# Softmax division of three batches moved to ScalarE and GpSimd with one folded factor, and an earlier start of some weight sums, in a fused attention and feed-forward kernel

## The chip, the cores and the metric

The kernel runs on one core of a Trainium2 chip. A core has a matrix engine (TensorE, PE in the profile, whose weight loads are listed as PEld), a vector engine (VectorE, DVE), a scalar engine (ScalarE, ACT), GpSimd (POOL) and SyncE (SP), which here issues the DMA transfers. The metric is device time in microseconds, as the median of several executions. One further execution is taken with the hardware profiler, and all rows below come from it.

## What is computed

Four batches of eight heads of causal attention with a memory term are computed, and the result goes, as 2304 tokens of 512 features, through two gated feed-forward blocks. All data are fp32. Cut to what matters:

```python
# attention, per batch and head: S = 576, D = 64
scores = where(causal, -1e9, q @ k.T / sqrt(D))
a = exp(scores - scores.max(-1));  a /= a.sum(-1) + 1e-9
local = a @ v
q_p = phi(q)                                  # elu(q) + 1
mem_out = (q_p @ M_prev) / (q_p @ z_prev + 1e-6)
g = 1 / (1 + exp(-beta))                      # one number per head
x = g * mem_out + (1 - g) * local             # 2304 x 512
# block 1: w1, w2 512x1024, w3 1024x1024, w_out 1024x512
x = ((x @ w1) * (x @ w2)) @ w3 @ w_out
# block 2: w_gate, w_val 512x1536, w_out 1536x512
out = (sigmoid(x @ w_gate) * (x @ w_val)) @ w_out
```

## The kernel before

**Batches and overlap.** The work goes batch by batch. `attention(b)` is a generator over 4 pairs of heads `p` and 5 row tiles `i` of 116 rows; row tile `i` sees 116(i+1) columns because of the causal mask, so its probabilities are 116x116 up to 116x580. `ffn(b)` is a generator over the feed-forward blocks of batch b. `drive` alternates the steps of `ffn(b)` with those of `attention(b+1)`, so the attention of batches 1, 2 and 3 runs inside the feed-forward work of batches 0, 1 and 2; the attention of batch 0 runs alone at the start, beside the preparation of weights. While `ffn(b)` is driven, `phase["n"]` is min(b+1, 3).

**Who sets the order.** PE's and SP's instructions stand in the order in which the program writes them. VectorE, ScalarE and GpSimd execute theirs in the order that the framework's scheduler gives, which places each instruction by the scheduler's own times. An engine executes its list in order: an instruction that waits holds back all behind it.

**The attention of one row tile.** PE writes the scores `s` of both heads of a pair to PSUM (L1177). VectorE adds the mask and takes the row minimum of the negated scores into `sm` (L1184, two reductions, `p<-s,msk`), which frees the PSUM bank for the next scores. ScalarE takes the exponential in place and sums it into `sm[:, 4:6]` (L137). `n_part` divides: VectorE adds 1e-9 (L1207) and takes the reciprocal (L1208) of both heads' sums, then each head's probabilities are multiplied in place by the reciprocal and by 1-g (L1210), on the engine that `lower(SHARE_N)` gives. With

```python
SHARE_N = (1.0, 0.5, 0.5, 0.5)
def lower(share):
    owed[share] = owed.get(share, 0.0) + share[phase["n"]]
    if owed[share] >= 1.0:
        owed[share] -= 1.0
        return nc.gpsimd
    return nc.vector
```

both heads of batch 0 go to GpSimd; of later batches the head 0 (`p_x_x_0`) goes to VectorE and the head 1 (`p_x_x_1`) to GpSimd. PE then transposes the divided probabilities (L1240, `t<-idf,p`) for the product with v, and ScalarE or VectorE copies the transposed blocks out of PSUM (L1258, `pt`, `pq`).

The memory term's `q` rows come by DMA (`qnr`); VectorE begins its share with `me` (L1107), reduces it (L1114 to L1117, `mn`) and multiplies (L1121, `mphi`).

**The feed-forward blocks.** A product is taken in several passes of high and low parts. In batch 0 and in some of batch 1 the fp32 weights are prepared on the way: ScalarE takes two pieces `cy`, `cr` of a loaded row `r` (L402, L403), VectorE joins them (L411), ScalarE casts the high part into a weight slot (`wslot`, L721) and VectorE subtracts (L723). From batch 2 on the first products of a block run on 16 bit weights with fewer passes: seven products (`abp`, `gvp`) are combined on VectorE and ScalarE into two halves of a row (`s1ab`, `s5ab`, `c11ab` copies on ScalarE; `u2ab`, `u3ab` L603 to L631 and `hraw` L594 on VectorE).

**Weight sums.** Those 16 bit weights are made in a list of `tasks` while PE is busy with the batches before. A task loads a kept fp32 unit by DMA (512 KB), and makes of it a part "P", or sums "S" (four VectorE additions on the unit, L433 to L436, then a scaled high part `wS` on ScalarE, L180, and a low part on VectorE, L181, then a DMA store), or both ("PS"). `late_split` does one step of a task: "P" one step, "S" two, "PS" three. It is called by every `ws["pace"]`-th `pump()`, and `pump()` is called after every second group of three matmuls of a product, so that 96 pumps lie in the gate and val products of batch 1 (L960, `gsb` on ScalarE, `hgraw` on VectorE). `ws["limit"]` is the number of tasks that may be begun: in that stretch it is `NPARTS`, which covers the last eight tasks "PS", and after it `NSUMS`, which covers twelve tasks "S" of the gate and val weights behind them.

Of the kernel before, what the change touches and what calls it, by code (L numbers as in the profile page):

```python
# [7 lines left out]
F32 = mybir.dt.float32  # L8
# [6 lines left out]
AF = mybir.ActivationFunctionType  # L15
ALU = mybir.AluOpType
AX = mybir.AxisListType

B, H, S, D = 4, 8, 576, 64
T = 116  # L20
# [21 lines left out]
SHARE_N = (1.0, 0.5, 0.5, 0.5)  # L42
# [12 lines left out]
FRAC = (0.96, 0.96, 0.96, 1.0)  # L55
FA = (1.0, 0.6)
FR0 = (0.75, 1.0)
PACE = (4, 4, 4, 14, 4, 8, 4)
WAIT = 4.0
AHEAD = (400, 0, 0, 0)  # L60

# [2 lines left out]
def tile_attention_memory_ffn(  # L64
# [17 lines left out]
    nc = tc.nc  # L82

    cp = ctx.enter_context(tc.tile_pool(name="cp", bufs=1))
# [20 lines left out]
    wmax = cp.tile([128, F1], F32, name="wmax")  # L105
    g = cp.tile([128, H], F32, name="g")
    omg = cp.tile([128, H], F32, name="omg")
    owed = {}
    phase = {"n": 0}

# [7 lines that stand above are left out]
    def turn(share):  # L118
        return lower(share) is nc.gpsimd
# [126 lines left out]
    NPARTS = len(tasks)  # L246
    tasks += [(u, "S") for u in jobs[:F2]]
    NSUMS = len(tasks)
# [23 lines left out]
    ws = {"conv": 0, "step": 0, "split": 0, "ring": 0, "freed": 0, "use": 0, "again": 0, "pumps": 0, "late": 0, "task": 0, "part": 0, "limit": 0, "pace": 0, "tops": 0, "wo": 0, "pass": 0, "wready": False}  # L272
# [38 lines left out]
    def late_scales():  # L311
        power(wsc[:, :NJ], wsc[:, NJ:], total("wsum", mcol[:, 0, :NJ], mcol[:, 1, :NJ]))
        nc.vector.tensor_reduce(wmax, wtop.rearrange("p d f -> p f d"), AX.X, ALU.max)
        nc.vector.tensor_reduce(wval, mcol[:, 1, :F2], AX.X, ALU.max)

    def o2_scale():
        col = bcol[:, 2 * B : 2 * B + 1]
        nc.vector.tensor_reduce(col, mcol[:, :, NJ:], AX.XY, ALU.max)
        power(o2s[:, 0:1], o2s[:, 1:2], total("osum", col))
# [437 lines left out]
    def ffn(b):  # L757
# [3 lines left out]
        if b == 1:  # L761
            o2_scale()
            ws["limit"], ws["pace"] = NFIRST, PACE[5]
        if b == 2:
            ws["pace"] = PACE[3]
        if b > 0:
# [42 lines left out]
        if b == 2:  # L809
            ws["pace"] = PACE[4]  # L810
        if b == 1:
# [71 lines left out]
                return hg_scale(b, x2top[:, : 4 if b == 1 else 8], x2s)  # L883

        if b == 1:
            ws["limit"], ws["pace"] = NPARTS, PACE[1]
        hgs = oback = None

        def finish_hg(f, ht, hraw):
# [11 lines left out]
        for f in range(F2):  # L901
            if b == 3:
# [18 lines left out]
                if f % 4 == 3:  # L921
# [4 lines left out]
                    first = [steps[x] for x in ("p0", "t1", "p1", "t2", "p2")]  # L926
# [44 lines left out]
        if b == 0:  # L971
            late_scales()
            ws["limit"], ws["pace"] = F2, PACE[0]
        if b == 1:
            ws["limit"], ws["pace"] = NSUMS, PACE[2]
        if b == 2:
# [89 lines left out]
    def attention(b, lag):  # L1066
        first = b == 0
# [136 lines left out]
        def n_part(p, i):  # L1204
            w = T * (i + 1)
            ps_, sm = sp[p, i]
            nc.vector.tensor_scalar(sm[:, 4:6], sm[:, 4:6], 1e-9, None, ALU.add)  # L1207
            nc.vector.reciprocal(sm[:, 6:8], sm[:, 4:6])  # L1208
            for hh in range(2):
                lower(SHARE_N).tensor_scalar(  # L1210
                    ps_[hh][:, :w], ps_[hh][:, :w], sm[:, 6 + hh : 7 + hh],
                    omg[:T, 2 * p + hh : 2 * p + hh + 1], ALU.mult, ALU.mult,
                )

        def t_parts(p, i):
            js = list(range(i + 1))
# [126 lines left out]
        for k in range(NPAIR * NT + lag):  # L1343
# [3 lines left out]
            if k < NPAIR * NT:  # L1347
                p, i = divmod(k, NT)
# [29 lines left out]
            if kk >= 0 and kk % NT == NT - 1:  # L1378
                p = kk // NT
# [25 lines left out]
    def setup():  # L1405
        nc.gpsimd.memset(msk[:, : SP - T], 0.0)
        nc.sync.dma_start(out=msk[:, SP - T :], in_=mask)
        bt = cp.tile([128, H], F32, name="bt")
        nc.sync.dma_start(out=bt, in_=beta)
        nc.sync.dma_start(out=idf, in_=ident)  # L1410
        nc.vector.memset(ones, 1.0)
        nc.gpsimd.memset(mcol[:, 1, F2:NJ], 0.0)
        nc.scalar.activation(out=g, in_=bt, func=AF.Exp, scale=-1.0)
        nc.vector.tensor_scalar(g, g, 1.0, None, ALU.add)
        nc.vector.reciprocal(g, g)
        nc.vector.tensor_scalar(omg, g, -1.0, 1.0, ALU.mult, ALU.add)

    def start():
        for g in range(NPREP):
            yield from prep(g)  # L1420
# [19 lines left out]
    with tc.manual_schedule(engines={mybir.EngineType.SP}):  # L1440
        next(a0)
        setup()
        load64(0)
        next(a0)
        load64(1)
        next(a0)
        for n in range(2, R64):
            load64(n)
# [82 lines left out]
```

## Time and profile before

| | before |
|---|---|
| median of 3 executions | 1018.73 us (1015.56 to 1020.03) |
| profiled execution | 1015.14 us, of which 1013.2 us from the first to the last instruction |
| PE granted clock, mean | 0.989 of full speed |
| PE busy | 980.7 us (97% of the span) |
| VectorE busy | 741.8 us (73%) |
| ScalarE busy | 595.8 us (59%) |
| GpSimd busy | 196.4 us (19%) |

The times of the rows are microseconds from the span's start. The attention of batch 1 lies, with gaps, at 100 to 360 us, that of batch 2 at 390 to 600 us, that of batch 3 at 620 to 830 us. The gate and val products of batch 1 lie at 498 to 573 us.

### The profile page before, as it was taken

The numbers are of one execution on the slowest core, as the hardware profiler recorded it, in microseconds if no ns is written. First come the engines' busy times: TensorE is split into PE (matmuls) and PEld (weight loads), VectorE is DVE, ScalarE is ACT, GpSimd is POOL, SyncE is SP. The second block draws the span as 40 slices with busy tenths as digits, with TensorE's granted clock in tenths as the row PEclk, the third lists the DMA queues.
The fourth block names the chain that finished last, engine by engine and source line by source line (L and its number), as shares of the span: only waits on it lengthen the run. The fifth ranks groups of instructions, "written<-read, shape, count | busy, mean of one in ns | idle before, by whom it ended". The sixth has DMA issues, their size and how long they took to land. (4 is left out here: it accounts for less than half of the span.)

```text
span 1013.2 us, 19855 instructions
## 1 busy us (share of the span) xinstructions
PE 980.7 (97%) x7351; PEld 798.6 (79%) x7351; DVE 741.8 (73%) x1702; ACT 595.8 (59%) x1213; POOL 196.4 (19%) x196
## 2 busy tenths in 40 slices
PE   7999989999999999999999999999999999999998
PEld 3455778888999899898977777768877677797776
DVE  6666879867788827777777668988876757737783
ACT  7887877557777735564655445555644644324451
POOL 4344112213000102321200011343111311201110
PEclk9799999999999999999999999999999999999999
DMA  8666799867677349877987577555655656556532
GB/s 296 202 217 206 263 352 310 311 210 266 227 245 245 126 144 382 273 240 241 303 309 240 185 244 262 186 186 187 199 180 176 199 159 203 176 176 254 183 130 78
DMA packets 95640, 227.18 MB, mean 224 GB/s; under 512 B 11192, under 2 KB 39992, under 8 KB 95288
## 3 DMA queue, kind: packets, MB, share of 16 engines
q1 hardware_dynamic: 95544, 225.93, 66.0%
q8 instruction: 57, 0.93, 0.4%
q14 instruction: 39, 0.32, 0.1%
HBM read 164.55 MB, written 61.34 MB: 223 GB/s over the span
## 5 line engine op out<-in xcount | busy, mean ns | idle before, releaser
L532 PEld LDWEIGHTS <-wslot 128*128 128x128 f16 x1680 | 163.1, 98 | 53.6 <-issue 12.2
L1210 POOL TENSOR_SCALAR p<-p,sm,omg 116x116 f32<-116x116 f32 (+4 forms) x100 | 89.1, 895 | 348.0 <-DVE sm L1208 210.7
L521 PE MATMUL gv<-x,wslot 128*128 128x288 f32 (+1 forms) x1152 | 147.5, 290 | 0.2 <-ACT gsb L137 0.2
L521 PEld LDWEIGHTS <-wslot 128*128 128x128 f16 x1152 | 111.2, 98 | 32.1 <-issue 4.5
L532 PE MATMUL gvp<-x,wslot 128*128 128x288 f16 x1008 | 125.1, 286 | 3.4 <-ACT x L180 1.6
L521 PE MATMUL ot<-hg,wslot 128*128 128x288 f16 (+1 forms) x864 | 117.4, 290 | 0.0
L521 PE MATMUL ab<-x,wslot 128*128 128x288 f32 x768 | 116.3, 302 | 0.0
L521 PE MATMUL xw<-h,wslot 128*128 128x288 f32 x768 | 113.2, 301 | 1.6 <-ACT h L721 0.9
L137 ACT ACTIVATE p<-p,sm 116x116 f32<-116x116 f32 (+4 forms) x160 | 92.9, 583 | 36.2 <-DVE sm L1184 35.7
L521 PEld LDWEIGHTS ab<-x,wslot 128*128 128x128 f32 x768 | 104.8, 190 | 5.0 <-issue 3.1
L521 PEld LDWEIGHTS xw<-h,wslot 128*128 128x128 f32 x768 | 104.3, 189 | 5.2 <-issue 2.0
L532 PE MATMUL abp<-x,wslot 128*128 128x288 f16 x672 | 87.3, 286 | 4.9 <-DVE u3ab L631 1.7
L1184 DVE CUSTOM_DVE_ANT_0 p<-s,msk 116x116 f32<-116x116 f32 (+4 forms) x160 | 67.2, 453 | 24.6 <-PE s L1177 24.6
L723 DVE TENSOR_TENSOR wslot<-wraw,wslot 128x512 fp32r<-128x512 f32 x76 | 53.9, 711 | 39.6 <-ACT wslot L721 39.3
L521 PEld LDWEIGHTS gv<-x,wslot 128*128 128x128 f32 x576 | 76.4, 188 | 0.5 <-ACT gsb L137 0.5
L1240 PE MATMUL t<-idf,p 116*116 116x116 f32 x480 | 68.8, 274 | 5.0 <-DVE p L1210 2.6
L1240 PEld LDWEIGHTS t<-idf,p 116*116 116x116 f32 x480 | 54.4, 139 | 19.4 <-issue 4.9
L402 ACT ACTIVATE cy<-r 128x512 f32<-128x512 f32 x76 | 51.1, 672 | 15.5 <-issue 6.6
L721 ACT CAST wslot<-wraw 128x512 fp32r<-128x512 f32 x76 | 47.0, 621 | 17.5 <-PE gv L521 7.4
L411 DVE SCALAR_TENSOR_TENSOR wraw<-cy,cr 128x512 int32<-128x512 int32 x76 | 53.4, 728 | 1.6 <-ACT cr L403 1.4
L1258 ACT COPY pt<-t 116x696 f32<-116x696 f32 (+2 forms) x74 | 47.2, 644 | 7.9 <-PE t L1240 7.7
L521 PE MATMUL wps<-wo,wslot 128*128 128x512 f32 x192 | 51.0, 404 | 0.0
(210 smaller groups left out, 1642.5 us busy)
## 6 DMA issues: line engine op xcount, KB each, us to landing
wslot<-k SPq DMA_DIRECT2D x40, 512.0 KB, 4.8
wslot<-ka SPq DMA_DIRECT2D x40, 512.0 KB, 4.4
wrawl<-kf SPq DMA_DIRECT2D x32, 512.0 KB, 6.5
wslot<-kb SPq DMA_DIRECT2D x40, 384.0 KB, 3.5
k<-wslot SPq DMA_DIRECT2D x24, 512.0 KB, 4.5
r<-in_gv_dram SPq DMA_DIRECT2D x24, 512.0 KB, 4.7
kf<-wraw SPq DMA_DIRECT2D x20, 512.0 KB, 3.1
ka<-wS SPq DMA_DIRECT2D x20, 512.0 KB, 4.4
```

Source lines behind the costliest of these rows:

```text
L137: ins = nc.scalar.activation(**kw)
L402: nc.scalar.activation(out=y, in_=hi, func=AF.Prelu, scale=2.0**-112, alpha=2.0**32)
L411: nc.vector.scalar_tensor_tensor(z, y, 3, tmp["r"], ALU.logical_shift_left, ALU.bitwise_or)
L521: paced["pe"] = nc.tensor.matmul(ps, w[:, wi, blk, :], x[:, xi, cols : cols + n], start=first and part == 0, stop=last and part == 2,)
L532: paced["pe"] = nc.tensor.matmul(ps, w[:, wi, blk + k, :], x[:, xi, k, :], start=not more and k == 0 and part == 0, stop=k == 1 and part == 2,
L721: nc.scalar.copy(dst[:, 0], src)
L723: eng.tensor_sub(dst[:, 1], src, dst[:, 0].bitcast(F32))
L1184: nc.vector.tensor_tensor_reduce(out=ps_[hh][:, c0:c1], in0=os_[hh][:, at : at + c1 - c0], in1=msk[:, SP - w + c0 : SP - w + c1], scale=-0 ...
L1210: lower(SHARE_N).tensor_scalar(ps_[hh][:, :w], ps_[hh][:, :w], sm[:, 6 + hh : 7 + hh], omg[:T, 2 * p + hh : 2 * p + hh + 1], ALU.mult, ALU ...
L1240: nc.tensor.transpose(tp[:T, c : c + T], src[hh][:, j * T : (j + 1) * T], idf[:T, :T])
L1258: nc.scalar.copy(to, got)
```

## The change

There are three edits. In `n_part`, for batches 1 to 3, one VectorE instruction of another form (`scalar_tensor_tensor`, L1217 of the changed file) forms (sum + 1e-9) x `iomg`, where `iomg` is 1/(1-g) per head, so that its reciprocal holds both factors; the two probability tiles are then multiplied by one number per row, the one of head 1 on GpSimd as before, the one of head 0 on ScalarE (L1226) in place of VectorE. In `setup`, `iomg` is made from beta with two small VectorE instructions and one exponential. In `ffn(1)`, ahead of the gate and val products, the pace goes from every 4th pump to every 3rd, and the limit from `NPARTS` to `NSUMS`.

```diff
-PACE = (4, 4, 4, 14, 4, 8, 4)
+PACE = (4, 3, 4, 14, 4, 8, 4)
...
         if b == 1:
-            ws["limit"], ws["pace"] = NPARTS, PACE[1]
+            ws["limit"], ws["pace"] = NSUMS, PACE[1]
...
         def n_part(p, i):
             w = T * (i + 1)
             ps_, sm = sp[p, i]
-            nc.vector.tensor_scalar(sm[:, 4:6], sm[:, 4:6], 1e-9, None, ALU.add)
+            if first:
+                nc.vector.tensor_scalar(sm[:, 4:6], sm[:, 4:6], 1e-9, None, ALU.add)
...
+                return
+            nc.vector.scalar_tensor_tensor(
+                sm[:, 4:6], sm[:, 4:6], 1e-9, iomg[:T, 2 * p : 2 * p + 2], ALU.add, ALU.mult
+            )
             nc.vector.reciprocal(sm[:, 6:8], sm[:, 4:6])
             for hh in range(2):
-                lower(SHARE_N).tensor_scalar(
-                    ps_[hh][:, :w], ps_[hh][:, :w], sm[:, 6 + hh : 7 + hh],
-                    omg[:T, 2 * p + hh : 2 * p + hh + 1], ALU.mult, ALU.mult,
-                )
+                by = sm[:, 6 + hh : 7 + hh]
+                if turn(SHARE_N):
+                    nc.gpsimd.tensor_scalar(ps_[hh][:, :w], ps_[hh][:, :w], by, None, ALU.mult)
+                else:
+                    nc.scalar.activation(out=ps_[hh][:, :w], in_=ps_[hh][:, :w], func=AF.Copy, scale=by)
...
+        nc.vector.tensor_scalar(iomg, bt, 80.0, None, ALU.min)
+        nc.scalar.activation(out=iomg, in_=iomg, func=AF.Exp)
+        nc.vector.tensor_scalar(iomg, iomg, 1.0, None, ALU.add)
```

PE's order is the same in both, row for row. VectorE loses 60 rows of L1210, ScalarE gains 60 of L1226 and the exponential for `iomg`, GpSimd keeps its rows. The scheduler's order of other instructions moves around these in some places. Line numbers of the changed file are higher: L138 there is L137 before, L403 is L402, L1271 is L1258, L1108 is L1107, L632 is L631, L595 is L594, L181 is L180.

ScalarE, attention of batch 1, pair 0, row tiles 2 and 3, beside the preparation of the weight row `r_29`; before:

```order
L402 ACTIVATE cy_1640<-r_29_1571 128x512
L403 ACTIVATE cr_1641<-r_29_1571 128x512
L137 ACTIVATE p_0_3_0_1508,sm_0_3_1510<-p_0_3_0_1508,sm_0_3_1510 116x464
L800 COPY asb_0_1_1547<-ab_0_1_0_1504 128x288
L721 CAST wslot_1557<-wraw_1444 128x512
L137 ACTIVATE p_0_3_1_1509,sm_0_3_1510<-p_0_3_1_1509,sm_0_3_1510 116x464
L1258 COPY pt_0_1269<-t_0_2_0_1539 116x2x3x116
L402 ACTIVATE cy_1676<-r_30_1595 128x512
```

and in the changed kernel:

```order
L403 ACTIVATE cy_1622<-r_28_1540 128x512
L404 ACTIVATE cr_1623<-r_28_1540 128x512
L138 ACTIVATE p_0_3_0_1512,sm_0_3_1514<-p_0_3_0_1512,sm_0_3_1514 116x464
L801 COPY asb_0_1_1551<-ab_0_1_0_1508 128x288
L722 CAST wslot_1561<-wraw_1448 128x512
L138 ACTIVATE p_0_3_1_1513,sm_0_3_1514<-p_0_3_1_1513,sm_0_3_1514 116x464
L403 ACTIVATE cy_1644<-r_29_1575 128x512
L404 ACTIVATE cr_1645<-r_29_1575 128x512
L1226 ACTIVATE p_0_2_0_1432<-p_0_2_0_1432,sm_0_2_1434 116x348
L1226 ACTIVATE p_0_3_0_1512<-p_0_3_0_1512,sm_0_3_1514 116x464
L403 ACTIVATE cy_1680<-r_30_1599 128x512
```

The first exponential of tile 3 now stands ahead of the pieces of `r_29`, and the division of tile 2, which was VectorE's, stands behind the second exponential of tile 3 and behind both pieces of `r_29`.

VectorE, attention of batch 3, memory term of pair 1 (`me_1`) beside the first combined row `u3ab_0`, `hraw_0` of batch 2's first block; before:

```order
L1121 TENSOR_TENSOR mphi_0_7888<-mphi_0_7888,mn_0_7889 116x640
L631 TENSOR_TENSOR u3ab_0_7925<-u3ab_0_7925,abp_0_4_7935 128x288
L594 SCALAR_TENSOR_TENSOR hraw_0_7831<-s5ab_0_7902,undo_7832,u2ab_0_7892 128x288
L1107 TENSOR_SCALAR me_1_8406<-qnr_1_8322 116x640
L594 SCALAR_TENSOR_TENSOR hraw_0_7831<-u3ab_0_7925,undo_7832,c11ab_0_7917 128x288
L603 TENSOR_TENSOR u2ab_1_7978<-abp_1_6_7970,s1ab_1_7968 128x288
```

and in the changed kernel:

```order
L1122 TENSOR_TENSOR mphi_0_7932<-mphi_0_7932,mn_0_7933 116x640
L1108 TENSOR_SCALAR me_1_8448<-qnr_1_8364 116x640
L632 TENSOR_TENSOR u3ab_0_7969<-u3ab_0_7969,abp_0_4_7979 128x288
L595 SCALAR_TENSOR_TENSOR hraw_0_7875<-s5ab_0_7946,undo_7876,u2ab_0_7936 128x288
L595 SCALAR_TENSOR_TENSOR hraw_0_7875<-u3ab_0_7969,undo_7876,c11ab_0_7961 128x288
L604 TENSOR_TENSOR u2ab_1_8022<-abp_1_6_8014,s1ab_1_8012 128x288
```

`me_1`, which reads the transfer `qnr_1`, stood behind L631 and the first L594 and now stands ahead of both.

ScalarE at the start of the gate and val products of batch 1 (`gsb_f_h` for feature block f, half h); before:

```order
L180 ACTIVATE wP_6429<-wrawl_6328,wsc 128x768
L137 ACTIVATE gsb_1_0_6414<-gv_1_0_0_6397,x2back_6008 128x288
L137 ACTIVATE gsb_1_1_6447<-gv_1_1_0_6434,x2back_6008 128x288
L180 ACTIVATE wS_6501<-wrawl_6328,wsc 128x1024
L137 ACTIVATE gsb_2_0_6486<-gv_2_0_0_6471,x2back_6008 128x288
L180 ACTIVATE wP_6536<-wrawl_6364,wsc 128x768
```

and in the changed kernel:

```order
L181 ACTIVATE wP_6398<-wrawl_6332,wsc 128x768
L138 ACTIVATE gsb_1_0_6422<-gv_1_0_0_6407,x2back_6012 128x288
L181 ACTIVATE wS_6455<-wrawl_6332,wsc 128x1024
L181 ACTIVATE wP_6488<-wrawl_6354,wsc 128x768
L138 ACTIVATE gsb_1_1_6459<-gv_1_1_0_6442,x2back_6012 128x288
L138 ACTIVATE gsb_2_0_6500<-gv_2_0_0_6481,x2back_6012 128x288
L181 ACTIVATE wS_6542<-wrawl_6354,wsc 128x1024
```

Ahead of `gsb_1_1` there now stand a sum `wS` and a part `wP`, which stood behind it. Over the whole stretch of 96 pumps, 24 steps of tasks become 32: after the eight tasks "PS", four tasks "S" are done there; these four lay in batch 2 before, between its first block's last products and its gate and val products.

## Rows read from the trace of the kernel before

**Rows 1.** The page: span, then busy time and instructions of each engine.

```profile
span 1013.2 us, 19855 instructions
PE 980.7 (97%) x7351; PEld 798.6 (79%) x7351; DVE 741.8 (73%) x1702; ACT 595.8 (59%) x1213; POOL 196.4 (19%) x196
```

**Rows 2.** Timeline of PE; in brackets idle time before a row and releaser.

```profile
128.58 0.64 PE L1240 MATMUL t<-idf,p 116*116 116x116 f32 x2 [2.64 <-DVE p L1210]
...
139.62 0.38 PE L1177 MATMUL s<-qkh 64*116 64x290 f32 x1 [1.10 <-DVE sm L1184]
...
225.03 0.53 PE L521 MATMUL xw<-h,wslot 128*128 128x288 f32 x2 [0.91 <-ACT h L721]
226.26 0.40 PE L521 MATMUL xw<-h,wslot 128*128 128x288 f32 x1 [0.70 <-DVE h L723]
...
631.78 0.41 PE L532 MATMUL abp<-x,wslot 128*128 128x288 f16 x2 [1.65 <-DVE u3ab L631]
634.43 0.77 PE L532 MATMUL abp<-x,wslot 128*128 128x288 f16 x5 [1.02 <-DVE u2ab L603]
...
725.59 0.65 PE L532 MATMUL gvp<-x,wslot 128*128 128x288 f16 x4 [0.45 <-DVE x L181]
729.94 0.28 PE L532 MATMUL gvp<-x,wslot 128*128 128x288 f16 x1 [0.76 <-ACT x L180]
730.84 0.40 PE L532 MATMUL gvp<-x,wslot 128*128 128x288 f16 x2 [0.50 <-DVE x L181]
```

**Rows 3.** Groups by line: the VectorE divisions; busy us, mean ns.

```profile
L1210 DVE TENSOR_SCALAR p<-p,sm,omg 116x116 f32<-116x116 f32 (+4 forms) x60 | 36.5, 609 | 1.3
```

**Rows 4.** Groups by shape: ScalarE's exponentials 348 wide.

```profile
L137 ACT ACTIVATE p<-p,sm 116x348 f32<-116x348 f32 x32 | 18.6, 585 | 11.4 <-DVE sm L1184 11.1
```

**Rows 5.** Timelines of VectorE and ScalarE, 127 to 132 us.

```profile
...
127.66 0.66 ACT L402 ACTIVATE cy<-r 128x512 f32<-128x512 f32 x1 [0.67 <-DMA r<-in_w3t_dram]
127.87 0.15 DVE L1208 RECIPROCAL sm<-sm 116x2 f32<-116x2 f32 x1
128.06 0.46 DVE L1210 TENSOR_SCALAR p<-p,sm,omg 116x348 f32<-116x348 f32 x1
...
130.25 0.70 ACT L137 ACTIVATE p<-p,sm 116x464 f32<-116x464 f32 x1
...
130.92 0.73 ACT L1258 COPY pt<-t 116x696 f32<-116x696 f32 x1
```

**Rows 6.** Timeline of VectorE, 626 to 634 us.

```profile
626.04 1.53 DVE L1207 TENSOR_SCALAR sm<-sm 116x2 f32<-116x2 f32 x1
...
631.28 0.45 DVE L631 TENSOR_TENSOR u3ab<-u3ab,abp 128x288 f32<-128x288 f32 x1
...
633.09 0.49 DVE L1107 TENSOR_SCALAR me<-qnr 116x640 f32<-116x640 f32 x1 [0.94 <-DMA qnr<-in_qn_dram]
...
633.92 0.45 DVE L603 TENSOR_TENSOR u2ab<-abp,s1ab 128x288 f32<-128x288 f32 x1
```

**Rows 7.** Stretches: us, PE, PEld, DVE, ACT, POOL busy, PEclk, DMA share, GB/s.

```profile
125.00:130.00 5.00, 2.36 (x15) 2.09 (x14) 3.48 (x10) 3.81 (x10) 0.80 (x1) 0.82 1.04 395
225.00:230.00 5.00, 4.27 (x22) 3.70 (x23) 3.22 (x11) 3.09 (x7) 1.35 (x1) 0.72 0.90 315
500.00:525.00 25.00, 25.00 (x207) 19.97 (x206) 18.97 (x37) 15.01 (x21) 0.00 (x0) 1.00 0.88 308
525.00:550.00 25.00, 25.00 (x206) 19.97 (x205) 18.46 (x32) 13.02 (x18) 0.00 (x0) 1.00 0.82 277
550.00:575.00 25.00, 25.00 (x207) 18.77 (x206) 16.23 (x28) 12.78 (x19) 0.54 (x1) 1.00 0.68 223
```

**Rows 8.** Groups by shape in 498 to 574 us: the weight sums.

```profile
L181 DVE SCALAR_TENSOR_TENSOR wS<-wrawl,wsc,wS 128x1024 f16<-128x1024 f32 x7 | 9.0, 1285 | 2.2 <-ACT wS L180 2.2
L434 DVE TENSOR_TENSOR wrawl<-wrawl 128x256 f32<-128x256 f32 x7 | 3.0, 424 | 0.2
L180 ACT ACTIVATE wS<-wrawl,wsc 128x1024 f16<-128x1024 f32 x7 | 8.0, 1148 | 4.3 <-DVE wrawl L436 4.3
```

More of the change, by code (lines that the diff above doesn't have):

```diff
@@ L107, in tile_attention_memory_ffn @@
     omg = cp.tile([128, H], F32, name="omg")
+    iomg = cp.tile([128, H], F32, name="iomg")
     owed = {}
@@ L1206, in n_part @@
             ps_, sm = sp[p, i]
-            nc.vector.tensor_scalar(sm[:, 4:6], sm[:, 4:6], 1e-9, None, ALU.add)
+            if first:
+                nc.vector.tensor_scalar(sm[:, 4:6], sm[:, 4:6], 1e-9, None, ALU.add)
+                nc.vector.reciprocal(sm[:, 6:8], sm[:, 4:6])
+                for hh in range(2):
+                    lower(SHARE_N).tensor_scalar(
+                        ps_[hh][:, :w], ps_[hh][:, :w], sm[:, 6 + hh : 7 + hh],
+                        omg[:T, 2 * p + hh : 2 * p + hh + 1], ALU.mult, ALU.mult,
+                    )
+                return
+            nc.vector.scalar_tensor_tensor(
+                sm[:, 4:6], sm[:, 4:6], 1e-9, iomg[:T, 2 * p : 2 * p + 2], ALU.add, ALU.mult
+            )
             nc.vector.reciprocal(sm[:, 6:8], sm[:, 4:6])
             for hh in range(2):
-                lower(SHARE_N).tensor_scalar(
-                    ps_[hh][:, :w], ps_[hh][:, :w], sm[:, 6 + hh : 7 + hh],
-                    omg[:T, 2 * p + hh : 2 * p + hh + 1], ALU.mult, ALU.mult,
-                )
+                by = sm[:, 6 + hh : 7 + hh]
[3 more added lines that the diff above has]
+                    nc.scalar.activation(out=ps_[hh][:, :w], in_=ps_[hh][:, :w], func=AF.Copy, scale=by)
         def t_parts(p, i):
```

## The prediction

> **What bounds the kernel now.** I read the page first, for which engine is busy. PE works 980.7 us of a span of 1013.2 us [rows 1], so it stands idle 32.5 us in all, and PE's instructions and their order are the same in both kernels. A change can therefore bring no more than a part of those 32.5 us, apart from what PE's clock gives; what it costs has no such bound. VectorE, with 741.8 us, and ScalarE, with 595.8 us, have room on average [rows 1], so moving work from the one to the other matters only where PE waits for one of them. So the second view is PE's own timeline, for the rows that have a wait in brackets. Nine of them [rows 2] carry this prediction, 9.73 us together. They lie in four places: 2.64 us for the VectorE division of row tile 2 at 128.58 and 1.10 us at 139.62; 0.91 and 0.70 us at 225 to 226 for a cast on ScalarE and the subtraction behind it; 1.65 and 1.02 us at 631 to 634 for the combined rows on VectorE; 0.45, 0.76 and 0.50 us at 725 to 731 at the start of batch 2's gate and val products. The reader is to see that only the first is a wait for the instruction that the change moves. Third, the stretches [rows 7] show where PE has no wait to give: 25.00 us busy of 25 in each of the three windows from 500 to 575 us, the gate and val products of batch 1.
>
> The profiled execution took 1015.14 us, 1.9 us more than its span and 3.6 us under the median of the three, 1018.73. My sum is a difference from the profiled execution, and I put it on the median.
>
> **The division.** VectorE loses 60 divisions, 36.5 us, 609 ns each [rows 3]. ScalarE gains 60 instructions that no row of before shows. From below, nothing forbids that they are as short as the 0.46 us of the VectorE division 348 wide [rows 5]; from above, the exponential of the same tile takes 585 ns at 348 columns [rows 4], and a plain multiplication without accumulation should not be dearer. I take about 0.5 us at the mean width of 348: 30 us over the kernel, between 28 and 35. That takes ScalarE from 59% to 62%. Its sum costs PE nothing where a division has one of PE's products as cover; the order decides where it has none. GpSimd's divisions stay where they are, one multiplication shorter; no row shows that form, so I bound it between no gain and a third of a division, and take nothing, because head 0 and not head 1 is what PE waits for at 128.58. The new instruction on `sm` has two columns like the one it replaces, but reads `iomg` too. L1207 took 1.53 us at 626.04, against 0.15 us of the reciprocal on the same two columns [rows 5, 6], so something beside it holds it at times. If the new form is never held, 1.4 us come back on VectorE at such a place; if it is, nothing changes. I take nothing, since at 626 the list then waits for a transfer anyway (below).
>
> At tile 2 of batch 1, before, VectorE's reciprocal at 127.87 is followed by the division at 128.06, 0.46 us, and PE starts at 128.58. On ScalarE the pieces `cy`, `cr` of `r_29`, two exponentials, a copy and a cast fill 127.66 to 130.92, when the copy `pt` begins; the 0.67 us ahead of 127.66 were a wait for the load of `r_29` [rows 5]. The changed list holds the same six instructions, in another order, ahead of the division. If the first exponential fills the 0.67 us of waiting, they end at 130.25, if not at 130.92; with 0.5 us of division PE starts at 130.75 to 131.42 instead of 128.58. That is 2.2 to 2.8 us; I take 2.6, because the cast behind the exponential needs a row that VectorE joins only then. Behind it stand the division of tile 3, two pieces and the `pt` copy. Something comes back: the next wait, 1.10 us at 139.62, is for VectorE's reduction, which does not depend on this product, and a PE that arrives later waits less. From nothing to 1.1 comes back; I take 0.7. Net +1.9 us, range +1.1 to +2.8. The granted clock of 125 to 130 is 0.82 on the mean, with 2.36 us of PE work [rows 7]: some of it ran at 1.2 GHz around the wait, and a longer wait can put as much again there, 0.18 × 2.36 = 0.4 us, which I leave inside that range.
>
> In four more places the new order puts the division of tile 0 behind the exponential of tile 1's second head or behind a cast. Each costs at most about one exponential, 0.585 us [rows 4], so 0 to 2.3 us; I take +1.0. In the other 55 the transposition comes a product or more behind the division, and I cost them at nothing; where that cover is gone, the price is again one division, 0.5 us.
>
> At 225 us the cast of the last `h` row now stands ahead of four pieces of weight rows that it followed, and VectorE's half of that row ahead of two joins. PE's 0.91 us should go, and a part of the 0.70 us: −1.2 us, between 0 and −1.6. The granted clock of 225 to 230 is 0.72 on the mean, with 4.27 us of work [rows 7], so part of that work ran at 1.2 GHz after the wait. If the clock stayed at 2.4 GHz, up to 0.28 × 4.27 = 1.2 us more would come back. I take none of it, because other waits near it stay; the low end of the range has it.
>
> At 631 us a wait is added ahead of something. VectorE's `me_1` waited for its transfer up to 633.09 [rows 6]. It now stands ahead of L631, which ran at 631.28 and released PE at 631.78. Two divisions and their neighbours ahead of it have left VectorE, but the transfer does not come earlier: its issue on SP stands where it stood. So L631 starts at about 633.55, PE at about 634.0, and its next release, which needed the row that began at 633.92, comes behind L631 and two L594 rows, at about 635.3 instead of 634.43. Most of the loss swallows the second wait: +0.9 us at the end of the two. If the transfer lands 2 us earlier, 0.8 us are won instead; bounds −0.8 and +0.9. I take +0.9.
>
> **The earlier weight sums.** One "S" task is four additions of 424 ns and a low part of 1285 ns on VectorE, 3.0 us, and 1148 ns on ScalarE [rows 8], besides a load and a store of 0.5 MB each. Four of them move from about 695 to 733 us into the gate and val products of batch 1. There VectorE goes from 18.97 + 18.46 + 16.23 = 53.7 us of 75 to 65.6 (87%), and ScalarE from 40.8 to 45.4 (61%) [rows 7]. PE is covered by the three banks its products rotate through, and it waited for nothing there. The list shows one place where the cover is thin, a `wS` and a `wP` ahead of `gsb_1_1`. The lower bound is nothing, the upper four sums on ScalarE at 1.15 us, 4.6 us. I take +0.5, nearer to nothing, because both engines keep at least a tenth of their time free. On the DMA side, a task "PS" loads 0.52 MB and stores 0.39 and 0.52 MB, 1.44 MB from the tile sizes. Eight in 56 us instead of 75 are 51 GB/s more, so 308 becomes 359 and 277 becomes 328 GB/s. The stretch 125 to 130 us moved 395 GB/s [rows 7], so by that row they fit, and the weights of PE's products come in time. The Trainium skill (SBUF — State Buffer, section "A bandwidth-pool intuition that's wrong (but worth ruling out)") gives about 358 GB/s between HBM and one core. By that figure the first window, at 359, would have no room, and I would give the third rival below 0.15 in place of 0.07; the row of 395 GB/s disagrees with it and decides.
>
> Where the tasks leave, the three waits at 725 to 731 us, 1.71 us, lie beside ScalarE and VectorE work of just these sums; I take −1.5 us, between 0 and −1.7.
>
> Elsewhere VectorE's lower load shortens small waits: −0.7 us, between 0 and −2.
>
> **Sum.** +1.9 + 1.0 − 1.2 + 0.9 + 0.5 − 1.5 − 0.7 = +0.9 us, so 1016.0 us for an execution like the profiled one and 1019.6 us on the median. Since the profiled execution was quicker than all three of the others, I go a little under that: 1018 us. With every term at its low end the sum is −5.0, and −6.2 with the clock, 1012.5 on the median; with every term at its high end +10.6, 1029.
>
> **Rivals.** First, VectorE's relief is the larger thing. The division at 128 us comes in time because the scheduler's list lets ScalarE run ahead, and 60 divisions less let the combined rows come early. Then the waits at 225, 631 to 634 and 725 to 731 go, 1.61 + 2.67 + 1.71 = 6.0 us, and 0.7 elsewhere: 1012 us, and with the clock at 225 and the wait of 1.10 us at 139.62 gone too, 1010. For it speaks that VectorE is the engine behind most of [rows 2]; against it, that `me_1` now stands ahead of the very row at 631.
>
> Second, slower: a division held behind weight preparation on ScalarE. In batch 1's attention ScalarE's list mixes divisions with pieces `cy` that wait for loads, while the DMA engines are full, share 1.04 in 125 to 130 us [rows 7]. A piece that waits holds the division, and PE holds its whole list. The price is 2.6 us for each such place. At one place I have counted it; from three places on it decides, 7.8 us less 0.7 for the wait that shrinks, with the other terms at −1.0: +6.1, 1025 us. Against it speaks that most divisions there have several us of cover.
>
> Third, gate and val of batch 1. The four sums take their full 4.6 us from PE: 0.9 − 0.5 + 4.6 = +5.0, 1023.7 us. Against it, the free time of both engines.
>
> Fourth, nothing of it reaches PE, since PE is idle 3% of the span: 1018.7 us, inside my forecast.
>
> **Chances.** A measurement of this kernel can tell about 0.5% from no change, 5.1 us here: below 1013.6 is faster, above 1023.8 slower. My forecast, with the fourth, has 0.56; the first rival 0.25, the second 0.12, the third 0.07, half of it at the border. So faster 0.26, same 0.55, slower 0.19. The range that leaves out 2 in 10 reaches over the first two rivals, from 1010 to 1026 us; the forecast alone would be 1014 to 1023.
>
> **What would show it.** Right: PE's wait for tile 2 near 128 us has ScalarE's L1226 as its releaser and is 4 to 5.5 us instead of 2.64; the waits at 225 and at 725 to 731 are gone; VectorE's busy time falls by about 35 us and ScalarE's rises by about 30; the wait near 631 is longer, with L632 behind a wait for `qnr`. Wrong would be a PE wait in the gate and val products of batch 1, divisions on ScalarE far from 0.5 us, or PE's idle total moving by more than 5 us in either direction.

## The result, and the profile after

The change is slower: 1031.23 us median of 4 executions (1028.08 to 1038.44), against 1017.14 us of before (1014.3 to 1020.03, 4 executions with the three already shown). The ratio is 1.0150 with a 95% interval of 1.0114 to 1.0186, so 14 us, far outside the forecast of 1010 to 1026 us. The profiled execution took 1028.08 us. The page begins:

```profile
span 1026.3 us, 19900 instructions
PE 984.3 (96%) x7351; PEld 799.9 (78%) x7351; DVE 713.5 (70%) x1644; ACT 625.7 (61%) x1274; POOL 213.7 (21%) x196
```

Beside [rows 1] the reader is to see what did not move: PE's work is the same to 3.6 us. ScalarE gained 29.9 us, as forecast; VectorE lost 28.3, where about 35 were forecast. GpSimd gained 17.3 us, which was not forecast: it has the same number of instructions, with one multiplication less in 60 of them.

Since PE executes the same 7351 instructions in the same order, the start of each can be set beside its start before. Their lag grows to +12.9 us by the end, in these stretches (before's time):

| stretch | change of the lag | what PE waits for there in the changed kernel |
|---|---|---|
| 100 to 150 us | +1.9 | division of tile 2 on ScalarE |
| 150 to 190 | +0.5 | another division on ScalarE |
| 190 to 198 | +1.1 | division on GpSimd |
| 198 to 248 | +0.6 | a combined row at 225, a division |
| 348 to 365 | +2.9 | VectorE's reductions |
| 385 to 395 | +0.8 | division on ScalarE |
| 500 to 520 | +1.9 | `gsb` on ScalarE, gate and val of batch 1 |
| 575 to 600 | +0.4 | a division |
| 626 to 660 | +2.2 | `u3ab` on VectorE, behind the transfer `qnr` |
| 660 to 720 | +0.2 | |
| 720 to 745 | −0.9 | the three waits of before are two |
| 790 to 835 | +1.2 | divisions, most on GpSimd |

These are single executions, and the clock alone can move a stretch: over the first 100 us, which the change hardly touches, the profiles of the runs below lie between −3.6 and +0.8 us against before. So the table says where PE waits, and only roughly what a place costs.

PE's timeline of the changed kernel, its waits there (in brackets idle time and releaser):

```profile
130.81 0.45 PE L1253 MATMUL t<-idf,p 116*116 116x116 f32 x1 [5.05 <-ACT p L1226]
...
200.75 0.32 PE L1253 MATMUL t<-idf,p 116*116 116x116 f32 x1 [1.16 <-POOL p L1224]
...
230.25 0.40 PE L522 MATMUL xw<-h,wslot 128*128 128x288 f32 x1 [1.30 <-DVE h L724]
...
354.68 0.39 PE L1178 MATMUL s<-qkh 64*116 64x290 f32 x1 [2.17 <-DVE sm L1185]
...
399.07 0.41 PE L1253 MATMUL t<-idf,p 116*116 116x116 f32 x2 [1.28 <-ACT p L1226]
...
521.43 0.77 PE L522 MATMUL gv<-x,wslot 128*128 128x288 f16 x5 [1.10 <-ACT gsb L138]
...
643.48 0.88 PE L533 MATMUL abp<-x,wslot 128*128 128x288 f16 x3 [3.20 <-DVE u3ab L632]
...
742.05 0.40 PE L533 MATMUL gvp<-x,wslot 128*128 128x288 f16 x2 [0.76 <-ACT x L181]
...
742.91 0.28 PE L533 MATMUL gvp<-x,wslot 128*128 128x288 f16 x1 [0.45 <-DVE x L182]
```

The row at 130.81 answers to the one at 128.58 of [rows 2], 643.48 to 631.78, and 354.68 to this row of before, which was not among them:

```profile
349.29 0.76 PE L1177 MATMUL s<-qkh 64*116 64x290 f32 x2 [0.84 <-DVE sm L1184]
```

The rows at 521.43 and 200.75 stand where PE waited for nothing, or 0.03 us, before.

PE's granted clock is the second part. The stretches at three of those waits (us, PE, PEld, DVE, ACT, POOL busy, clock, DMA share, GB/s):

```profile
128.00:131.00 3.00, 0.19 (x1) 0.20 (x2) 2.21 (x5) 3.00 (x7) 1.92 (x2) 0.50 1.03 408
...
353.00:356.00 3.00, 1.32 (x8) 0.93 (x9) 3.00 (x8) 0.28 (x2) 0.90 (x1) 1.00 0.46 175
356.00:359.00 3.00, 3.00 (x18) 3.00 (x17) 3.00 (x7) 2.35 (x4) 1.42 (x1) 0.57 0.00 0
643.00:646.00 3.00, 2.52 (x11) 1.62 (x11) 2.98 (x7) 1.07 (x2) 0.00 (x0) 0.53 0.29 119
```

and before, behind the waits of 0.84 us at 349.29 and 1.65 us at 631.78:

```profile
351.00:354.00 3.00, 3.00 (x27) 3.00 (x25) 3.00 (x8) 2.87 (x6) 1.44 (x1) 1.00 0.46 175
631.00:634.00 3.00, 1.63 (x12) 1.17 (x12) 2.06 (x6) 0.40 (x1) 0.00 (x0) 1.00 0.98 385
```

Behind the wait of 2.17 us at 354.68 PE works three full microseconds at a mean clock of 0.57, so nearly all of it at 1.2 GHz; behind the 3.20 us at 643.48 at 0.53. Before, the same work behind the shorter waits ran at 1.00. It is not so each time: in the run e1 below, the same wait of 2.17 us (at 355.33) is followed by a clock of 1.00 (357 to 360 us), and in e5 two waits of 0.78 and 0.67 us there are followed by 0.52 (347 to 350 us).

Over all executions the mean granted clock is 0.9845 in the changed kernel, and 0.9907 to 0.9919 in the executions of before that ran beside the experiments, by chip. The difference, 0.0062 to 0.0074 of about 1015 us, is up to 7 us (an estimate from above, since PE also stands idle in some of that time, as in 128 to 131 us). In the two profiled executions, from which the lags come, it is 0.986 against 0.989, at most about 3 of the 12.9 us.

### The profile page after: what moved, and what is told of

It is laid out like the page before. It is cut to its first block, busy times and chain, and to the rows that moved or that the text cites. A ratio compares the mean times of both kernels' runs of the same rounds, so it can differ in the third digit from the quotient of the medians.

```text
span 1026.3 us, 19900 instructions
## 1 busy us (share of the span) xinstructions
PE 984.3 (96%) x7351; PEld 799.9 (78%) x7351; DVE 713.5 (70%) x1644; ACT 625.7 (61%) x1274; POOL 213.7 (21%) x196
## 5 line engine op out<-in xcount | busy, mean ns | idle before, releaser
L1224 POOL TENSOR_SCALAR p<-p,sm 116x116 f32<-116x116 f32 (+4 forms) x60 | 75.0, 1251 | 299.2 <-DVE sm L1220 211.2
L138 ACT ACTIVATE p<-p,sm 116x116 f32<-116x116 f32 (+4 forms) x160 | 93.2, 585 | 32.7 <-DVE sm L1185 32.6
L412 DVE SCALAR_TENSOR_TENSOR wraw<-cy,cr 128x512 int32<-128x512 int32 x76 | 54.0, 737 | 2.7 <-ACT cr L404 2.4
L403 ACT ACTIVATE cy<-r 128x512 f32<-128x512 f32 x76 | 51.5, 678 | 6.7 <-DVE wraw L412 3.1
L1271 ACT COPY pt<-t 116x696 f32<-116x696 f32 (+2 forms) x74 | 47.4, 646 | 8.1 <-PE t L1253 8.0
```

Source lines behind the costliest of these rows:

```text
L138: ins = nc.scalar.activation(**kw)
L403: nc.scalar.activation(out=y, in_=hi, func=AF.Prelu, scale=2.0**-112, alpha=2.0**32)
L412: nc.vector.scalar_tensor_tensor(z, y, 3, tmp["r"], ALU.logical_shift_left, ALU.bitwise_or)
L1224: nc.gpsimd.tensor_scalar(ps_[hh][:, :w], ps_[hh][:, :w], by, None, ALU.mult)
L1271: nc.scalar.copy(to, got)
```

## The experiments

My theory after the profile: the loss is a sum over places, in which ScalarE's divisions come late, GpSimd's new form is slow, and the scheduler's new order on VectorE delays two things that PE waits for; the longer waits then cost the clock as well. Rivals: the weight sums are most of it; GpSimd's form is most of it; ScalarE's 60 instructions more delay everything a little. All ratios are against before on the same chip, with 95% intervals; the clock is the mean granted clock over the timed executions.

| run | division, head 0 (batches 1, 2, 3) | GpSimd's form | sums early | median us | ratio | clock |
|---|---|---|---|---|---|---|
| the change | ScalarE | one factor | yes | 1031.23 | 1.0150 (1.0114 to 1.0186) | 0.9845 |
| e1 | ScalarE | one | no | 1030.11 | 1.0136 (1.0111 to 1.0160) | 0.9860 |
| e2 | as before | two, as before | yes | 1016.45 | 1.0003 (0.9982 to 1.0025) | 0.9913 |
| e3 | ScalarE | two | yes | 1026.13 | 1.0099 (1.0064 to 1.0133) | 0.9882 |
| e4 | VectorE | one | yes | 1023.51 | 1.0063 (1.0037 to 1.0089) | 0.9896 |
| e5 | VectorE | two | yes | 1017.99 | 1.0026 (1.0006 to 1.0046) | 0.9911 |
| e6 | ScalarE, six tiles VectorE | two | yes | 1022.34 | 1.0076 (1.0050 to 1.0102) | 0.9871 |
| e7 | ScalarE, `me_1` on GpSimd | one | yes | 1029.61 | 1.0138 (1.0109 to 1.0167) | 0.9848 |
| e9 | VectorE, VectorE, ScalarE but two tiles | two | yes | 1018.15 | 1.0024 (1.0002 to 1.0047) | 0.9910 |
| e10 | ScalarE, VectorE, VectorE | two | yes | 1024.70 | 1.0086 (1.0057 to 1.0114) | 0.9876 |
| e11 | VectorE, ScalarE, VectorE | two | yes | 1018.60 | 1.0014 (0.9988 to 1.0039) | 0.9908 |
| e12 | ScalarE but two tiles, VectorE, VectorE | two | yes | 1018.60 | 1.0026 (1.0002 to 1.0049) | 0.9930 |

**The two halves of the change (e1, e2).** e1 takes the weight sums back, e2 keeps them alone:

```diff
 # e1, from the change; e2 is the reverse, from before
-PACE = (4, 3, 4, 14, 4, 8, 4)
+PACE = (4, 4, 4, 14, 4, 8, 4)
...
-            ws["limit"], ws["pace"] = NSUMS, PACE[1]
+            ws["limit"], ws["pace"] = NPARTS, PACE[1]
```

> The change with its two numbers for the weight sums put back (pace 4, limit NPARTS), so the division alone. Theory: the loss of about 14 us is a sum of waits that the division makes in many places (ScalarE late with head 0, GpSimd late with head 1, VectorE's new order at 349 and 631 us); the sums cost 1.9 us in gate and val of batch 1 and give back 0.9 us at 725 us. Then this takes about 1030 us, at most 1 to 2 us less than the change, and PE has no wait in gate and val of batch 1. Rival: the four earlier sums are most of the loss, by the transfers that they crowd; then this takes 1017 to 1022 us.

> The kernel before with only the two numbers for the weight sums changed (pace 3, limit NSUMS). Theory: +1.9 us of PE waits for gsb in gate and val of batch 1, -0.9 to -1.7 us at 725 us, so 1017 to 1019 us, no difference that can be told. Rival (the sums are most of the loss): 1025 us or more.

The division alone makes the time 1.0136 of before; the sums alone change nothing that can be told (1.0003, 0.9982 to 1.0025; the median, 1016.45 us, is a little under the theory's 1017 to 1019). PE's waits of e2 in 498 to 580 us, grouped (us in total, times, longest):

```profile
PE gv L521 <- ACT gsb L137: 1.3, 2, 0.9
```

So the sums do cost PE a wait where it had none, 1.3 us here, and give 0.9 us back at 725 us: the lags there are +1.6 and −0.9 in e2, +1.9 and −0.9 in the change, and nothing at both places in e1. The rival that they are the loss is out.

**GpSimd's form and ScalarE's share (e3, e4, e5).** e3 gives GpSimd's instruction a second factor, a column of ones; e4 puts head 0 back on VectorE; e5 does both:

```diff
 # e3, e5
-                    nc.gpsimd.tensor_scalar(ps_[hh][:, :w], ps_[hh][:, :w], by, None, ALU.mult)
+                    nc.gpsimd.tensor_scalar(ps_[hh][:, :w], ps_[hh][:, :w], by, one[:T, 0:1], ALU.mult, ALU.mult)
 # e4, e5
-                    nc.scalar.activation(out=ps_[hh][:, :w], in_=ps_[hh][:, :w], func=AF.Copy, scale=by)
+                    nc.vector.tensor_scalar(ps_[hh][:, :w], ps_[hh][:, :w], by, None, ALU.mult)
```

> The change with GpSimd's division given a second factor, a column of ones, so that its instruction has the form of before (two multiplications); result and order stay as in the change. Theory: GpSimd's instruction 348 wide goes back from 1.16 to 0.80 us, PE's waits for GpSimd go from 2.8 to under 1 us, and some of VectorE's held time comes back: 1026 to 1029 us, 2 to 5 us less than the change. Rival: the slower form on GpSimd is the main cause, since it also holds VectorE: 1017 to 1022 us. Second rival: GpSimd's time does not reach PE: 1031 us.

> The change with head 0 divided on VectorE by the folded factor (one multiplication), nothing of it on ScalarE; GpSimd as in the change. Theory: PE's waits for ScalarE's divisions, 8.0 us, go, VectorE's order is near that of before, and the GpSimd form and the sums stay: about 1021 to 1025 us. Rival (the GpSimd form is the main cause): 1028 us or more. Second rival (only ScalarE's late divisions matter): 1017 to 1019 us.

> Head 0 back on VectorE (folded factor, one multiplication) and GpSimd with its second factor of ones: nothing of the division on ScalarE, GpSimd's form as before; the folded sum and the earlier weight sums stay. Theory (the loss is the sum of a ScalarE part of about 6.5 us and a GpSimd part of about 4 us): 1017 to 1020 us, within 0.4% of before. Rival (the two are not additive; what is left is the folded sum on VectorE and the new order): 1022 us or more.

GpSimd's divisions by shape (busy us, mean ns), 348 wide before:

```profile
L1210 POOL TENSOR_SCALAR p<-p,sm,omg 116x348 f32<-116x348 f32 x12 | 11.2, 937 | 83.6 <-DVE sm L1208 56.8 <-ACT x L180 8.5 <-PE ot L521 7.9
```

in the change:

```profile
L1224 POOL TENSOR_SCALAR p<-p,sm 116x580 f32<-116x580 f32 x12 | 21.6, 1801 | 19.7 <-DVE sm L1220 8.7 <-DVE wrawl L436 6.8 <-ACT wslot L722 2.2
...
L1224 POOL TENSOR_SCALAR p<-p,sm 116x348 f32<-116x348 f32 x12 | 14.7, 1224 | 86.0 <-DVE sm L1220 68.1 <-PE ot L522 7.5 <-ACT asb L801 4.8
```

and in e3, the same data by two factors:

```profile
L1225 POOL TENSOR_SCALAR p<-p,sm,one 116x580 f32<-116x580 f32 x12 | 10.8, 897 | 21.1 <-DVE sm L1221 8.7 <-DVE wrawl L437 7.5 <-ACT wslot L723 2.8
...
L1225 POOL TENSOR_SCALAR p<-p,sm,one 116x348 f32<-116x348 f32 x12 | 8.4, 704 | 90.8 <-DVE sm L1221 77.4 <-PE ot L523 7.9 <-ACT pq L1274 3.6
```

The instruction with one factor takes longer than the one with two: 1801 against 897 ns at 580 columns, 1224 against 704 at 348. Before, with VectorE's divisions beside it, 348 columns took 937. A mean has waiting in it; the shortest of each twelve took 1734 against 827 ns at 580 columns, 1154 against 634 at 348 and 570 against 441 at 116, so about 2.5 against 0.83 ns for each further column.

The four runs make a square. With head 0 on ScalarE, GpSimd's form is worth 0.0051 of the time (change to e3); on VectorE 0.0037 (e4 to e5): about 4 to 5 us. ScalarE instead of VectorE is worth 0.0087 with one factor (e4 to the change) and 0.0073 with two (e5 to e3): about 7 to 9 us. By the intervals of the runs each of these differences can be off by 0.003 to 0.005. As far as that can tell the two add up, and what is left in e5 is 0.0026. All three times came out within the theory's ranges.

The way was not the theory's. PE's waits for GpSimd's divisions were to fall from 2.8 to under 1 us in e3, and they stayed at 2.8 us. What fell is the wait for `u3ab`. PE's waits, grouped (us in total, times, longest), in the change and in e3:

```profile
PE abp L533 <- DVE u3ab L632: 3.2, 1, 3.2
PE t L1253 <- POOL p L1224: 2.8, 6, 1.2
...
PE t L1256 <- POOL p L1225: 2.8, 3, 2.2
PE abp L534 <- DVE u3ab L633: 1.1, 1, 1.1
```

So most of the GpSimd part is not GpSimd's time. In the change, e1 and e4, with one factor, the scheduler sets `me_1` ahead of `u3ab`, and the lag over 626 to 660 us is +2.2, +2.6 and +2.5 us. In the runs with two factors it sets `u3ab` first again, as before, and that lag is −0.2 to −1.5. Between the change and e3 these are 3.7 us, between e4 and e5 2.8. How much of the 4 to 5 us would be left with the order put right is open.

**One wait on VectorE (e7).** The change's VectorE at 640 to 643 us:

```profile
640.50 0.82 DVE L1122 TENSOR_TENSOR mphi<-mphi,mn 116x640 f32<-116x640 f32 x1
642.57 0.49 DVE L1108 TENSOR_SCALAR me<-qnr 116x640 f32<-116x640 f32 x1 [1.25 <-DMA qnr<-in_qn_dram]
642.98 0.45 DVE L632 TENSOR_TENSOR u3ab<-u3ab,abp 128x288 f32<-128x288 f32 x1
```

L632 stood ready behind `me_1`, which waited 1.25 us for the transfer. e7 takes `me_1` off VectorE's list:

```diff
-            nc.vector.tensor_scalar(e, q_, 0.0, None, ALU.min)
+            (nc.gpsimd if (b, p) == (3, 1) else nc.vector).tensor_scalar(e, q_, 0.0, None, ALU.min)
```

> The change, but the first step of the memory term of batch 3, pair 1 (me_1), is done on GpSimd, so that VectorE's list no longer waits for the transfer qnr_1 there. Theory: PE's wait of 3.2 us near 643 us falls to about 1.5, and the stretch at the lower clock behind it goes: 1027 to 1029 us, 2 to 4 us less than the change. Rival (the combined rows are late for VectorE's other work, not for the transfer): 1031 us.

PE's row there in e7:

```profile
649.59 2.61 PE L533 MATMUL abp<-x,wslot 128*128 128x288 f16 x20 [1.46 <-DVE u3ab L632]
```

The wait goes from 3.20 to 1.46 us, as expected, and the lag over 626 to 640 us from +1.8 to −1.5. The median falls by 1.6 us, to just above the theory's 1027 to 1029 us, and less than the intervals can tell: the mechanism is shown in the profile, its worth in the whole is not.

**Where ScalarE's part lies (e6, e9, e10, e11).** e6 returns to VectorE the six tiles for which PE waited on ScalarE; the others use ScalarE in one batch only:

```diff
 # from e3
-                else:
+                elif (b, p, i) in LATE:                       # e6: six tiles
+                elif (b, p, i) in LATE or b < 3:              # e9: (3, 2, 4), (3, 3, 0)
+                elif b != 1:                                  # e10; e11: b != 2
+                    nc.vector.tensor_scalar(ps_[hh][:, :w], ps_[hh][:, :w], by, None, ALU.mult)
+                else:
                     nc.scalar.activation(out=ps_[hh][:, :w], in_=ps_[hh][:, :w], func=AF.Copy, scale=by)
```

> As the run with two factors on GpSimd, but the six divisions of head 0 for which PE waited on ScalarE (batch 1: pair 0 tile 2, pair 1 tile 0, pair 3 tile 0; batch 2: pair 0 tile 0; batch 3: pair 2 tile 4, pair 3 tile 0) are done on VectorE; the other 54 stay on ScalarE. Theory (ScalarE costs PE only where its list holds the division back): PE's waits for ScalarE's divisions go, 5 to 8 us with the clock: 1018 to 1021 us. Rival (54 divisions more on ScalarE delay its copies and casts all over the program): 1024 us or more.

> GpSimd with its second factor; head 0 on VectorE in batches 1 and 2, and on ScalarE in batch 3 alone, but for two tiles whose product comes at once. Theory: batch 3 has cover for its divisions and VectorE is what PE waits for there, so nothing is lost against the same kernel with all of head 0 on VectorE, and up to 3 us may be won: 1014 to 1018 us. Rival (ScalarE's copies of the combined rows come late for it): 1020 us or more.

> GpSimd with its second factor; head 0 on ScalarE in batch 1 alone, on VectorE in batches 2 and 3. Theory: nearly all of ScalarE's part, about 7 us against the same kernel with head 0 on VectorE (1018.0 us), is made in batch 1, where ScalarE also prepares weights and PE's waits at about 130, 225 and 350 us lie: 1023 to 1026 us. Rival (the part is spread evenly over the three batches): 1020 us.

> GpSimd with its second factor; head 0 on ScalarE in batch 2 alone, on VectorE in batches 1 and 3. Theory: one wait at about 395 us, 1 us, sometimes more with the clock: 1018 to 1020 us. Rival (spread evenly): 1020 us; if batch 2 is the place: 1023 us or more.

e6 was a miss: 1022.34 us, between theory and rival. Its grouped waits of PE in 100 to 870 us say why:

```profile
PE t L1259 <- DVE p L1230: 4.2, 2, 3.8
PE s L1180 <- DVE sm L1187: 3.8, 4, 2.2
```

The waits for ScalarE's divisions are gone, but one of 3.8 us for VectorE has taken the place of the one at 130 us, and the wait of 2.2 us for VectorE's reductions near 353 us is as in the change. It is no wait for a division, so the six tiles did not hold it. e10 and e11 then placed the part: batch 1 alone costs 0.0060 against e5, which the intervals tell from nothing; batch 2 costs nothing that can be told, and e9 says the same of batch 3. Nothing was won in batch 3 either (1018.15 us, the upper edge of the theory's 1014 to 1018), though VectorE is the engine that PE waits for there.

**Two divisions of 20 (e12).** In the change the scheduler sets two joins of weight rows (L412) ahead of the next reductions near 353 us; VectorE there:

```profile
351.59 0.17 DVE L1220 RECIPROCAL sm<-sm 116x2 f32<-116x2 f32 x1
...
352.63 1.63 DVE L412 SCALAR_TENSOR_TENSOR wraw<-cy,cr 128x512 int32<-128x512 int32 x2
354.17 0.45 DVE L1185 CUSTOM_DVE_ANT_0 p<-s,msk 116x290 f32<-116x290 f32 x1
```

Before, the division of pair 3 tile 3 stood on VectorE between the reciprocal and the reductions, and the joins behind them:

```profile
347.74 0.52 DVE L1210 TENSOR_SCALAR p<-p,sm,omg 116x464 f32<-116x464 f32 x1
...
348.77 0.45 DVE L1184 CUSTOM_DVE_ANT_0 p<-s,msk 116x290 f32<-116x290 f32 x1
...
349.53 1.29 DVE L411 SCALAR_TENSOR_TENSOR wraw<-cy,cr 128x512 int32<-128x512 int32 x2
```

PE's next scores need the bank that the reductions free. e12 is e10 with that tile and pair 0 tile 2 back on VectorE:

```diff
-                elif b != 1:
+                elif b != 1 or (p, i) in ((3, 3), (0, 2)):
```

> As the run with ScalarE in batch 1 alone, but two of its 20 divisions go back to VectorE: pair 0 tile 2 (the wait near 129 us) and pair 3 tile 3, whose place in the list lets two joins of weight rows stand ahead of the next reductions (the wait near 353 us). Theory (batch 1's part is made of a few places, and half of it is these two with the lower clock behind them): PE's wait near 129 us goes from 4.9 to about 2.6 us, that near 353 us from 2.2 to under 1.5 us, and the time is 1018.5 to 1021.5 us. Rival (the other 18 divisions cost as much each): 1023 us or more.

PE in e10:

```profile
129.90 1.41 PE L1258 MATMUL t<-idf,p 116*116 116x116 f32 x6 [4.88 <-ACT p L1231]
...
353.37 0.77 PE L1179 MATMUL s<-qkh 64*116 64x290 f32 x2 [2.24 <-DVE sm L1186]
```

and in e12:

```profile
130.08 1.22 PE L1258 MATMUL t<-idf,p 116*116 116x116 f32 x5 [3.58 <-DVE p L1229]
...
355.74 0.39 PE L1179 MATMUL s<-qkh 64*116 64x290 f32 x1 [0.76 <-DVE sm L1186]
...
356.80 0.39 PE L1179 MATMUL s<-qkh 64*116 64x290 f32 x1 [0.67 <-DVE sm L1186]
```

The wait near 353 us falls from 2.24 to 0.76 and 0.67 us, as expected; the one near 130 us only to 3.58, not to 2.6, and it is now VectorE's. The time falls from 1.0086 to 1.0026, as in e5, where nothing is divided on ScalarE. So the other 18 divisions of batch 1 cost nothing that can be measured. No run has one of the two tiles back alone. e6 had pair 0 tile 2 on VectorE and pair 3 tile 3 on ScalarE, and was still 0.0050 above e5, which points to pair 3 tile 3 as the larger.

The waits shrink by 2.1 us in these profiles, the median by 6.1 us; the mean clock rises from 0.9876 to 0.9930 (before's, beside them, were 0.9907 and 0.9916), which is up to 5.5 us. That the clock is the rest fits the numbers, but the profiled execution of e12, with a span of 1023.1 us, is the longest of its twelve, and its rows do not show it: behind the short waits near 356 us the clock still fell, to 0.71 over 356 to 359 us, and the lag over 340 to 366 us is +2.2, against +3.0 in e10. Also, e10 lost 2.9 us at 385 to 396 us (before's time), by a wait of 1.18 us for a division on VectorE in batch 2, which e12 does not have. So the times show that the two tiles together make batch 1's part; that they make all of it at their own two places is not shown.

## Why the prediction was wrong

Three terms that the sum took at nothing failed most: GpSimd's new form, one place of the division (pair 3 tile 3), and the clock. The rows add many small ones: of the 12 us between the sum's +0.9 and the lag of +12.9, 2.9 lie near 353 us, 3.6 where a relief of 0.7 was taken and 2.9 were lost (198, 575 to 600, 660 to 720 and 790 to 835 us), 1.4 in gate and val, 1.3 at 631 us, 1.2 at 225 us, 0.9 in other tiles and 0.6 at 725 us. All went the same way.

**GpSimd's price was the step that failed first.** I bounded GpSimd's new form "between no gain and a third of a division", which has no side on which it costs, and took nothing. No row of before showed the form; that the instruction is one multiplication shorter was a reason and not a measurement. It takes longer, 1154 instead of 634 ns at 348 columns where nothing holds it, and it costs 4 to 5 us of the kernel (e3, e4, e5). It gets there less by waits for GpSimd than by the order of `me_1` and `u3ab`, so in the rows most of this price lies at 631 us.

**ScalarE's price was right, its first place too.** Its divisions at 348 columns:

```profile
L1226 ACT ACTIVATE p<-p,sm 116x348 f32<-116x348 f32 x12 | 7.0, 583 | 2.0 <-DVE sm L1220 2.0
```

That is the upper bound that I named, 585 ns [rows 4], and the mean over the five widths, 586 ns, makes 35 us, the top of 28 to 35. At tile 2 the list runs as worked out:

```profile
128.39 0.68 ACT L138 ACTIVATE p<-p,sm 116x464 f32<-116x464 f32 x1
...
129.07 0.65 ACT L403 ACTIVATE cy<-r 128x512 f32<-128x512 f32 x1
129.63 0.65 ACT L404 ACTIVATE cr<-r 128x512 int32<-128x512 uint32 x1
130.19 1.14 ACT L1226 ACTIVATE p<-p,sm 116x348 f32<-116x348 f32 x2
```

The exponential, the two pieces, the division (two are joined in the last row): PE starts at 130.81, inside 130.75 to 131.42; the wait is 5.05 us against 4 to 5.5; and 0.8 us come back at 139.62, against 0.7 taken. The lag is +1.9, as in the sum, with 0.3 of it from a longer stretch at the lower clock, which the sum had only in its range.

**The 55 places "at nothing" held one that was not.** For pair 3 tile 3 the division itself had cover. What it had done on VectorE was to hold two joins behind the reductions. Taken off, the order there turned, and PE's wait of 0.84 us became 2.17, +2.9 us with the clock. I had looked for late divisions and not for what moves into their place. By e12 this tile and tile 2 together carry batch 1's part, 6 us of the time, where the sum had 1.9.

**Of the four other tiles** three came out at +1.9 us in the lags (150 to 190, 241 and 385 to 395 us), against +1.0 taken and 2.3 as the bound for all four. A fourth such wait, 0.60 us at 815 us, stands where PE waited 0.96 us before.

**At 225 us** the wait of 0.91 us did not go: PE waits 0.89 us for the combined row on VectorE, and the wait behind it grew from 0.70 to 1.30, with another of 0.57 us for the reductions at 231 us [rows 2]. That is 1.15 us more, where the sum had −1.2. The stretch still came out at 0, by the clock that the sum had left out: 0.72 over 225 to 230 us before [rows 7], 1.00 over 224 to 236 us in the change.

**At 631 us** the mechanism was right, even to VectorE's L632 behind `qnr`; the size was off, +2.2 instead of +0.9 us: the wait grew from 1.65 to 3.20 us, and PE then worked at a clock of 0.53.

**Gate and val of batch 1** cost +1.9 us, against +0.5 taken and 4.6 as the bound, by the thin place that the text named, `gsb_1_1`; 725 us gave back 0.9 of 1.5. Both together, +1.0 us, lie within e2's interval. The transfers fit, as the prediction had it: 353 GB/s over 500 to 525 us, against 359 worked out, and PE's waits there are for `gsb` alone.

**VectorE's relief elsewhere**, −0.7, did not come. Where head 1 on GpSimd was covered by head 0 before, it is the later one now, 1.1 us at 198 us alone. That one is not the form: in e3, with two factors, PE waits 2.20 us for GpSimd there, behind the same `me` of 1.55 us.

**The clock was left at nothing** in the sum except as a gain at 225 us. Up to half of the 14 us is there. Each wait was priced at its own length, and a longer wait brought slower work behind it in many of the profiles, if not in each.

The forecast's second rival, slower by a division held on ScalarE, had the sign and one of its places; its count of like places was wrong, since the loss near 353 us is another mechanism and GpSimd's form was in no rival.

What stays open: the 0.0026 of e5, 2.6 us, is the folded sum on VectorE with the order that goes with it, or the one-factor form on VectorE; e2 without both is 1.0003, and the intervals of the two overlap. No run divides these, but VectorE's division by one factor took 461 to 608 ns by shape in e5, against 543 to 778 before, so its length is not it. No version here is faster than before; e2, e5, e9, e11 and e12 are within 0.3% of it. Open too is how much of the change's 14 us is the clock and how much of GpSimd's 4 to 5 us is the order near 631 us.

## What to carry to other kernels

When work leaves an engine whose order a scheduler makes, look not only at when the moved instruction ends but at what the old engine now does sooner: two of 20 moved divisions made the loss of a batch, and in the profile one is late and one no longer stands in front of something else. Price a form of an instruction that the trace doesn't show from both sides, also when it does less arithmetic, and look again at the order that the scheduler makes with it. And where PE is nearly always busy, a wait can cost its length and then the clock behind it: near 353 us a wait that grew by 1.3 us cost 2.9 us in one execution, and 1.35 in another (e1), where the clock held.

## What the runs showed of the hardware that I had not expected

GpSimd's `tensor_scalar` with one per-row factor is slower than with two: the shortest of twelve took 570 to 1734 ns over 116 to 580 columns, against 441 to 827 ns with a second factor of ones (the change and e3). The Trainium skill (SBUF — State Buffer, section "SBUF: two separate sides") says that VectorE and GpSimd share a pair of ports, and that whichever comes first, a GpSimd instruction or a VectorE instruction that reads two inputs from SBUF, has it for its whole length while the other waits. The trace agrees for the pair of them: in the change, L1217 on VectorE, which reads `sm` and `iomg`, took 1.52 us from 636.32 beside a GpSimd instruction of 1.54 us from 636.28, against 0.16 us in the median of its 60. At 116 columns the mean with two factors is the longer one, 917 against 784 ns: beside VectorE's `mphi` (L1111 in the change) these instructions took about 1080 ns with two factors and 575 with one. The price of the form with one factor is not such a wait, since the shortest of each twelve differ too.

The granted clock was 0.57 and 0.53 for 3 us behind waits of 2.17 and 3.20 us, and 1.00 behind the waits of 0.84 and 1.65 us at the same places before. The length of the wait alone does not decide it: behind 2.17 us it was 1.00 in e1, and behind 0.78 and 0.67 us it was 0.52 in e5.
